# Attention and two mixtures on one core: which queue issues the DMAs inside the first mixture's branches

## The chip, the cores and the metric

One core of a Trainium2 chip runs the whole program in one launch. The metric is the device time of one execution in microseconds (us). Five engines work beside each other: TensorE (PE, matmuls), VectorE (DVE), ScalarE (ACT), GpSimd (POOL) and SyncE (SP, which here only issues DMAs). Each runs its own instruction stream in program order and waits on semaphores for the others. "SPq", "ACTq" and "POOLq" in a profile are those engines' queues of DMA, register, branch and semaphore instructions.

## The reference, cut to what matters

An attention within chunks of 64 tokens gives x, a matrix of N = 2304 tokens by 512. Two mixtures follow.

```
# first mixture: each token goes to one of 8 experts, with a capacity of 2N/8 = 576 tokens an expert
expert = argmax(x @ w_gate)
gate   = softmax(x @ w_gate)[expert]
y[i]   = gate[i] * relu(x[i] @ w1[expert[i]]) @ w2[expert[i]]     # 0 if over capacity
# second mixture: every token through every expert, weighted by P, a matrix normalised 8 times over rows and columns
P   = exp(y @ w2_gate), then 8 x (rows to sum 1, columns to sum 1, times N/8)
out = sum over e of P[:, e] * relu(y @ w21[e]) @ w22[e]
```

How many tokens an expert of the first mixture gets depends on the data, so the kernel decides at run time how many blocks of rows it works on.

## The kernel before, in words

Matrices are split into a high and a low fp16 part and multiplied three times. The first stage (to about 142 us of the profile) is the attention, the routing and the writing of all token rows to a DRAM buffer `xs_d`; it also leaves in `reg_i` the token count `rc` and the first rank `rb` of each expert, and in `gidx` the tokens of each expert. The second stage (142 to about 427 us) is the first mixture. The third stage (to the end, 1868 us) is the second mixture.

The loop of the first mixture (lines 789 to 862) goes over the experts x = 0 to 7 in turn, and each engine takes the instructions in the order in which they are written:

- GpSimd gathers tokens from `xs_d` by indirect DMA (`gather`, line 665): `late`, the third and fourth 128 tokens of expert x, and `rows`, the first 256 tokens of expert x+1. SyncE turns `rows` by two DMA transposes (`turn_dma`, line 674).
- The main block (`blocks(..., main=True)`, line 848) does the first 256 tokens of expert x. TensorE multiplies with w1 (line 718), ScalarE and VectorE make the hidden tiles hh and hl (lines 722, 723), TensorE turns `late` (`turn`, lines 683 to 686, called through `between`) and multiplies with w2 (line 735). Between the pieces, at `sites`, lie the splits of the next expert's weights (`w_split`, lines 216 to 218 and 224, 225, of which part runs on GpSimd), the loads of weights three experts ahead (`load_next`, line 153, on SyncE) and their statistics. For the last expert the sites hold `w_quad` (lines 240 to 250): GpSimd forms sums of the second mixture's first weights, ScalarE and VectorE split them.
- Each 128 rows of the result are written to the DRAM buffer `x2_d` (line 748, 256 KB) and their scale and token number to `rk_d` (line 753, 128 pairs of 8 bytes). The address is `rb + 128 t`, a register, so a write counts as touching any part of the buffer: each write to `x2_d` waits until the one before it has landed, and so with `rk_d`. Before line 748 GpSimd copies the token numbers into the pair (line 707).
- Then come the branches (lines 850 to 862): with more than 256 tokens a block for the third 128 (`Else`, line 862), with more than 384 a block for the third and fourth together (line 852), with more than 512 a loop for what is left (line 854), with a gather in it. In the profiled execution experts 0 and 2 take the block of two, experts 3 and 6 the block of one, experts 1, 4, 5 and 7 none: 16 + 6 blocks of 128 rows in all.
- For the last expert, `heads` (line 771) loads the first 768 rows of `x2_d` for the second mixture: ahead of the main block if these rows are already written (line 811; so it is here), else inside the innermost branch (line 860).

The DMAs of lines 748 and 753 are issued by SyncE, for the last expert by ScalarE; those of `heads` by SyncE. A side of a branch that issues fewer DMAs than the other, or none, makes up for them: it waits on each semaphore that the other side's DMAs would have raised and raises it itself, so that the count is the same behind the branch. These instructions stand in the profile under the lines of the branches (850, 851, 853): `EVENT_SEMAPHORE` on SyncE for the semaphores of SyncE's and ScalarE's DMAs, `INC_SWDGE_SEM` on GpSimd for those of GpSimd's. This text calls them pads.

The second mixture starts with `x_first` (line 930), whose matmuls read `heads` (line 943) and whose results go into tiles on the memory that the first mixture has left (lines 952, 961, 962).

Of the kernel before, what the change touches and what calls it, by code (L numbers as in the profile page):

```python
# [30 lines left out]
def kernel(ctx, tc, q, k, v, w_gate, w1, w2, capacity, w2_gate, w21, w22, out):  # L31
    nc = tc.nc
    B, H, S, D = q.shape
    N, DM = out.shape
    E, _, F = w1.shape
# [19 lines left out]
    x2_d = dram.tile([N + 256, DM], F32, name="x2_d")  # L55
# [11 lines left out]
    def sm(nm, shape, dtype=F32):  # L67
        return small_pool[-1].tile(shape, dtype, tag=nm, name=nm)
# [19 lines left out]
    def pow2_of_sumsq(ssq, log2, h, s, inv):  # L88
        nc.vector.tensor_scalar(out=h, in0=ssq.bitcast(I32), scalar1=24, scalar2=None, op0=ALU.logical_shift_right)
        nc.vector.tensor_scalar(out=s.bitcast(I32), in0=h, scalar1=-float(1 << 23), scalar2=float((189 + log2) << 23),  # L90
                                op0=ALU.mult, op1=ALU.add)
        nc.vector.tensor_scalar(out=inv.bitcast(I32), in0=h, scalar1=float(1 << 23), scalar2=float((65 - log2) << 23),
                                op0=ALU.mult, op1=ALU.add)
# [163 lines left out]
    for i in range(NS):  # L257
        r, done = [], 0
        while done < 256:
            b, s = divmod(i * 256 + done, S)  # L260
            n = min(256 - done, S - s)
# [6 lines left out]
    reg_i = const.tile([128, 2 * E], I32, name="reg_i")  # L268
    gidx = const.tile([128, E, NT], I32, name="gidx")
    NV = 4  # L270
    with ExitStack() as actx:
# [330 lines left out]
        for n in range(NT + 6):  # L602
# [13 lines left out]
            queue = []  # L616
# [6 lines left out]
            for f, lag in order:  # L623
# [5 lines left out]
                queue = queue[share:]  # L629
# [20 lines left out]
    with ExitStack() as cctx:  # L650
# [27 lines left out]
        def turn(rows, tag, bank="y"):  # L678
            xT = cp.tile([128, 2 * KD, 128 * len(rows)], F16, tag=tag, name=tag, bufs=2 if tag == "xT" else 1)
            for n, (idx, kg, xg) in enumerate(rows):  # L680
                p = ps_c.tile([128, 2 * KD, 128], F16, tag=bank, name="p_t", bufs=2 if bank != "p" else 3)
                for kk in range(2 * KD):
                    nc.tensor.transpose(p[:, kk, :], xg[:, kk * 128:(kk + 1) * 128], id16)
                sl = slice(n * 128, (n + 1) * 128)
                nc.scalar.copy(out=xT[:, 0:KD, sl], in_=p[:, 0:KD])
                nc.vector.tensor_copy(xT[:, KD:2 * KD, sl], p[:, KD:2 * KD])
            return xT, rows
# [3 lines left out]
        def blocks(x, pre, nb, row0, sites=(), main=False, between=None):  # L691
            a, b = mats[x, "a"], mats[x, "b"]
            xT, rows = pre
            W = 128 * nb
            sites = list(sites)

            def bank(nm, shape):
                tag, bufs = {"p": ("p", 3), "y": ("y", 2)}[nm] if main else ("c", 2)
                return ps_c.tile(shape, F32, tag=tag, name="p_" + nm, bufs=bufs)

            def site():
                for f in (sites.pop(0) if sites else ()):
                    f()

            tos = [sm("rkt", [128, 2]) for _ in range(nb)]
            for (idx, _, _), to in zip(rows, tos):
                nc.gpsimd.tensor_copy(to[:, 1:2].bitcast(I32), idx)
            hh = cp.tile([128, KF, 256], F16, tag="hh", name="hh", bufs=1)[:, :, 0:W]
            hl = cp.tile([128, KF, 256], F16, tag="hl", name="hl", bufs=1)[:, :, 0:W]
            FG = 512 // W  # L710
            for fg in range(KF // FG):
                p = bank("p", [128, FG, W])
                for f4 in range(FG):
                    f = fg * FG + f4
                    n = 0
                    for w, lo in ((a.hi, 0), (a.hi, KD), (a.lo, 0)):
                        for kk in range(KD):
                            nc.tensor.matmul(p[:, f4, :], lhsT=w[:, kk, f * 128:(f + 1) * 128], rhs=xT[:, lo + kk, 0:W],  # L718
                                             start=(n == 0), stop=(n == 3 * KD - 1))
                            n += 1  # L720
                fs = slice(fg * FG, fg * FG + FG)
                nc.scalar.activation(out=hh[:, fs, :], in_=p, func=AF.Relu)
                nc.vector.scalar_tensor_tensor(out=hl[:, fs, :], in0=p, scalar=0.0, in1=hh[:, fs, :],
                                               op0=ALU.max, op1=ALU.subtract)
                site()
            for t in range(nb):
                idx, kg, _ = rows[t]
                sl = slice(t * 128, t * 128 + 128)
                if t == 0 and between:
                    between()  # L730
                y = bank("y", [128, DM])
                n = 0
                for kk in range(KF):
                    for h, w in ((hh, b.hi), (hh, b.lo), (hl, b.hi)):
                        nc.tensor.matmul(y, lhsT=h[:, kk, sl], rhs=w[:, kk, :], start=(n == 0), stop=(n == 3 * KF - 1))  # L735
                        n += 1
                sq, ssq = cp.tile([128, DM], BF16, tag="sq", name="sq2", bufs=1), sm("ssq2", [128, 1])
                nc.scalar.activation(out=sq, in_=y, func=AF.Square, accum_out=ssq)
                s, inv = sm("x2s", [128, 1]), sm("x2i", [128, 1])
                pow2_of_sumsq(ssq, LX, sm("x2h", [128, 1], I32), s, inv)  # L740

                rhl = cp.tile([128, 2, 2, DM // 2], F16, tag="row", name="row2", bufs=3)
                yh = y.rearrange("p (c n) -> p c n", c=2)
                nc.scalar.activation(out=rhl[:, :, 0, :], in_=yh, func=AF.Copy, scale=s)
                nc.vector.scalar_tensor_tensor(out=rhl[:, :, 1, :], in0=yh, scalar=s, in1=rhl[:, :, 0, :],
                                               op0=ALU.mult, op1=ALU.subtract)
                queue = nc.scalar if x == E - 1 else nc.sync
                queue.dma_start(out=x2_d[bass.ds(row0(t), 128), :],
                                in_=rhl.rearrange("p c l n -> p (c l n)").bitcast(F32))
                to = tos[t]  # L750
                nc.vector.scalar_tensor_tensor(out=to[:, 0:1], in0=kg, scalar=inv, in1=iws[x],
                                               op0=ALU.mult, op1=ALU.mult)
                queue.dma_start(out=rk_d[bass.ds(row0(t), 128), :], in_=to)
                site()
            assert not sites
# [12 lines left out]

        head = []

        def heads():
            for n, (lo, hi) in enumerate(((0, 4), (4, 6))):
                if len(head) < 2:
                    head.append(wpool.tile([128, 4096], F16, tag=f"s{2 + n}", name=f"head{n}").bitcast(F32)
                                .rearrange("p (j c) -> p j c", c=DM))
                nc.sync.dma_start(out=head[n][:, 0:hi - lo, :],
                                  in_=x2_d[lo * 128:hi * 128, :].rearrange("(j p) c -> p j c", p=128))

        def tokens(x, *ts):
            return [gidx[:, x, t:t + 1] for t in ts]  # L780
# [8 lines left out]
        for x in range(E):  # L789
            y = x + 1  # L790
            rc = nc.values_load(reg_i[0:1, x:x + 1], min_val=0, max_val=N)
            rank_engine = mybir.EngineType.Activation if x == E - 1 else mybir.EngineType.SP
            rb = nc.values_load(reg_i[0:1, E + x:E + x + 1], engines=[rank_engine], min_val=0, max_val=N)

            def rank(t):
                return nc.s_assert_within(rb + t * 128, 0, N + 128,
# [2 lines left out]
            def ranks(t0):  # L799
                return lambda t: rb if t0 + t == 0 else rank(t0 + t)  # L800
# [7 lines left out]
                    loads(2, nm)  # L808
            if x == E - 1:
                with tc.If(rc <= N - SB):  # L810
                    heads()

            if y < E:
                for nm in "ab":
# [35 lines left out]
            with tc.If(rc > 256):  # L850
                with tc.If(rc > 384) as cmp:
                    blocks(x, (late_t, late_r), 2, ranks(2))
                    with tc.If(rc > 512):
                        with tc.For_i(4, (rc + 127) // 128, 1) as t:
                            idx = cp.tile([128, 1], I32, tag="idx", name="idx")
                            nc.vector.tensor_copy(idx, gidx[:, x, bass.ds(t, 1)])
                            blocks(x, turn(gather([idx]), "xTl", "c"), 1, lambda _: rank(t))
                        if x == E - 1:
                            with tc.If(rc > N - SB):
                                heads()  # L860
                with cmp.Else():
                    blocks(x, (late_t, late_r[:1]), 1, ranks(2))

# [258 lines left out]
    for x in range(E):  # L1122
# [36 lines left out]
        for s in range(NSB):  # L1159
            hs = [[ep.tile([128, SB], F16, tag=f"{nm}{f}", name=nm) for nm in ("eh", "el")] for f in range(KF)]  # L1160
            n = 0
# [15 lines left out]
            for t in range(6):  # L1177
                j = s * 6 + t
# [13 lines left out]
                if x == E - 1:  # L1192
                    nc.gpsimd.indirect_dma_start(out=out[:, :], out_offset=bass.IndirectOffsetOnAxis(ap=rk[:, j, 1:2].bitcast(I32), axis=0),
                                                 in_=acc[:, j, :], in_offset=None)
# [38 lines left out]
```

## Time and profile before

| | |
|---|---|
| runs of the kernel before | 1873.75, 1872.31, 1871.22 us (median 1872.31) |
| the profiled execution | 1869.98 us |
| its span, first to last instruction | 1868.3 us |
| PE / DVE / ACT / POOL busy, share of the span | 96% / 54% / 39% / 26% |
| mean granted TensorE clock | 0.982 of full speed (2.4 GHz) |

A row of a timeline gives the start and the length of a run of like instructions on one engine, and in square brackets how long the engine was idle before it and what it waited for. A row of the view of one line gives count, shortest, median and longest duration in ns, and the first and last start. Idle time of an engine that is not the bottleneck costs nothing by itself.

### The profile page before, as it was taken

The numbers are of one execution on the slowest core, as the hardware profiler recorded it, in microseconds if no ns is written. First come the engines' busy times: TensorE is split into PE (matmuls) and PEld (weight loads), VectorE is DVE, ScalarE is ACT, GpSimd is POOL, SyncE is SP. The second block draws the span as 40 slices with busy tenths as digits, with TensorE's granted clock in tenths as the row PEclk, the third lists the DMA queues.
The fourth block names the chain that finished last, engine by engine and source line by source line (L and its number), as shares of the span: only waits on it lengthen the run. The fifth ranks groups of instructions, "written<-read, shape, count | busy, mean of one in ns | idle before, by whom it ended". The sixth has DMA issues, their size and how long they took to land.

```text
span 1868.3 us, 27396 instructions
## 1 busy us (share of the span) xinstructions
PE 1785.7 (96%) x10757; PEld 1015.4 (54%) x10757; DVE 1013.1 (54%) x1978; ACT 721.0 (39%) x1310; POOL 479.1 (26%) x494
## 2 busy tenths in 40 slices
PE   7868999888999999999999999999999999999998
PEld 6756666655455555555545555555555555555553
DVE  4896657756566734654464545355534653464432
ACT  7964656644334333541233323233322431242210
POOL 1344336541012310421131113112301321042221
PEclk9988999989999999999999999999999999999999
DMA  9747556833342112130222113112112130212200
GB/s 232 204 154 225 157 177 162 220 112 126 91 121 78 60 45 104 60 105 9 96 85 80 60 47 104 60 60 105 46 60 102 63 105 1 105 59 72 82 34 35
DMA packets 135118, 182.11 MB, mean 97 GB/s; under 512 B 62240, under 2 KB 80752, under 8 KB 134960
## 3 DMA queue, kind: packets, MB, share of 16 engines
q1 hardware_dynamic: 127968, 162.22, 28.1%
q0 software_dynamic: 5360, 17.24, 2.9%
q8 instruction: 98, 1.61, 0.4%
q14 instruction: 60, 0.49, 0.1%
q10 hardware_dynamic: 1632, 0.56, 0.1%
HBM read 149.21 MB, written 23.56 MB: 92 GB/s over the span
## 4 chain that ended last, share of the span: by engine, by line
PE 69%; DVE 4%; ACT 3%; issue 1%; POOL 1%; DMA 0%; POOLq 0%; DVEq 0%
PE p_m L1116 39%; PE p_m L1054 29%; DVE c L1060 1%; ACT eh L1070 1%; DVE el L1071 1%; ACT wsq L164 1%; POOL w L1089 1%; PE p_m L943 0%; ACT m L1079 0%; ACT m L1099 0%; PE p_l L173 0%; DVE w L225 0%; DVE u L1060 0%; ACT w L224 0%; DMA out_dram<-acc,rk 0%
## 5 line engine op out<-in xcount | busy, mean ns | idle before, releaser
L1116 PE MATMUL p_m<-w,eh 128*128 128x512 f16 x2304 | 685.6, 379 | 2.5 <-ACT eh L1070 2.5
L1054 PE MATMUL p_m<-x,w 128*128 128x384 f16 x4032 | 665.1, 327 | 1.7 <-DVE c L1060 1.3
L1054 PEld LDWEIGHTS <-w 128*128 128x128 f16 x4032 | 395.0, 98 | 264.6 <-issue 4.9
L1116 PE MATMUL p_m<-w,el 128*128 128x512 f16 x1152 | 437.0, 379 | 0.0
L1116 PEld LDWEIGHTS <-eh 128*128 128x128 f16 x2304 | 225.2, 98 | 269.0 <-ACT eh L1070 3.7
L1089 POOL TENSOR_TENSOR w<-u,m 128x384 f32<-128x384 f32 x96 | 96.6, 1006 | 971.3 <-DVE u L1060 911.2
L1070 ACT ACTIVATE eh<-c 128x384 f16<-128x384 f32 x384 | 190.3, 518 | 402.3 <-DVE c L1060 402.3
L1190 DVE SCALAR_TENSOR_TENSOR acc<-p_m,cf,acc 128x512 f32<-128x512 f32 x126 | 94.6, 751 | 383.1 <-PE p_m L1116 376.9
L1071 DVE SCALAR_TENSOR_TENSOR el<-c,eh 128x384 f16<-128x384 f32 x384 | 218.3, 570 | 126.7 <-ACT eh L1070 116.1
L1079 ACT COPY m<-p_m 128x384 f32<-128x384 f32 x96 | 44.6, 465 | 400.3 <-PE p_m L1054 400.3
L1116 PEld LDWEIGHTS <-el 128*128 128x128 f16 x1152 | 112.7, 98 | 137.3 <-DVE el L1071 1.8
L718 PEld LDWEIGHTS <-w 128*128 128x128 f16 x1152 | 109.0, 102 | 30.5 <-issue 11.5
L735 PE MATMUL p_y<-w,hh 128*128 128x512 f16 x352 | 106.4, 384 | 0.0
L718 PE MATMUL p_p<-xT,w 128*128 128x256 f16 x768 | 91.3, 282 | 10.5 <-DMA xT<-xg 4.8
L1094 POOL TENSOR_TENSOR c<-u,m 128x384 f32<-128x384 f32 x96 | 95.7, 997 | 1.5 <-DVE u L1060 1.5
L1060 DVE TENSOR_TENSOR u<-p_m,m 128x384 f32<-128x384 f32 x96 | 53.4, 556 | 59.6 <-PE p_m L1054 59.6
L1060 DVE TENSOR_TENSOR c<-p_m,w 128x384 f32<-128x384 f32 x96 | 53.5, 558 | 49.9 <-PE p_m L1054 32.6
L249 ACT ACTIVATE w<-wsum,wsa 128x1024 f16<-128x1024 f32 x32 | 36.6, 1145 | 88.0 <-POOL wsum L243 88.0
L1060 DVE TENSOR_TENSOR u<-p_m,u 128x384 f32<-128x384 f32 x96 | 53.5, 558 | 27.8 <-PE p_m L1054 25.7
L735 PE MATMUL p_y<-w,hl 128*128 128x512 f16 x176 | 67.5, 384 | 1.1 <-issue 1.1
L164 ACT ACTIVATE wsq<-sta 128x1024 bf16<-128x1024 f32 x64 | 67.6, 1056 | 0.9
L225 DVE SCALAR_TENSOR_TENSOR w<-stb,wsb,w 128x1024 f16<-128x1024 f32 x46 | 62.9, 1379 | 6.2 <-ACT w L224 6.1
(236 smaller groups left out, 1663.3 us busy)
## 6 DMA issues: line engine op xcount, KB each, us to landing
x<-xt_d SPq DMA_DIRECT2D x147, 384.0 KB, 4.5
sta<-in_moe_w_dram SPq DMA_DIRECT2D x18, 1024.0 KB, 7.0
stb<-in_moe_w_dram SPq DMA_DIRECT2D x18, 1024.0 KB, 7.3
sta<-in_moe_w_dram SPq DMA_DIRECT2D x28, 512.0 KB, 8.7
stb<-in_moe_w_dram SPq DMA_DIRECT2D x28, 512.0 KB, 12.2
xt_d<-x SPq DMA_DIRECT2D x21, 384.0 KB, 3.1
x_d<-row SPq DMA_DIRECT2D x20, 256.0 KB, 4.6
vbd<-in_v_dram SPq DMA_DIRECT2D x72, 64.0 KB, 4.1
```

The costliest lines, as they stand in the source:

```text
L164: nc.scalar.activation(out=sq, in_=src, func=AF.Square, accum_out=m.mx[:, h:h + 1])
L225: nc.vector.scalar_tensor_tensor(out=m.lo[:, sl, :], in0=m.st[:, sl, :], scalar=m.s, in1=m.hi[:, sl, :], op0=ALU.mult, op1=ALU.subtract)
L718: nc.tensor.matmul(p[:, f4, :], lhsT=w[:, kk, f * 128:(f + 1) * 128], rhs=xT[:, lo + kk, 0:W], start=(n == 0), stop=(n == 3 * KD - 1))
L735: nc.tensor.matmul(y, lhsT=h[:, kk, sl], rhs=w[:, kk, :], start=(n == 0), stop=(n == 3 * KF - 1))
L1054: nc.tensor.matmul(p, lhsT=wt[:, w, lw, kk, :], rhs=xt[:, lx, kk, :], start=(n == 0), stop=(n == 5))
L1060: nc.vector.tensor_tensor(out=c, in0=p, in1=t, op=ALU.add)
L1070: nc.scalar.activation(out=hh[:, sl], in_=src, func=AF.Relu)
L1071: nc.vector.scalar_tensor_tensor(out=hl[:, sl], in0=src, scalar=0.0, in1=hh[:, sl], op0=ALU.max, op1=ALU.subtract)
L1089: nc.gpsimd.tensor_tensor(out=Q["w"], in0=Q["u2"], in1=Q["m5"], op=ALU.add)
L1094: nc.gpsimd.tensor_tensor(out=Q["c22"], in0=Q["u3"], in1=Q["m5"], op=ALU.add)
L1116: nc.tensor.matmul(y, lhsT=h[:, t * 128:(t + 1) * 128], rhs=w[:, kk, :], start=(n == 0), stop=(n == 3 * KF - 1))
L1190: nc.vector.scalar_tensor_tensor(out=acc[:, j, :], in0=y, scalar=coefs[x][:, j:j + 1], in1=acc[:, j, :], op0=ALU.mult, op1=ALU.add)
```

## The change

In the branches every DMA is issued by GpSimd; the main blocks' writes of all experts, the last one's too, by SyncE. `heads` is issued by GpSimd at both places. The first rank `rb` is loaded into registers of SyncE and of GpSimd for every expert (before: SyncE, for the last expert ScalarE). SyncE then has no instruction inside a branch.

```diff
-                queue = nc.scalar if x == E - 1 else nc.sync
+                queue = nc.sync if main else nc.gpsimd
                 queue.dma_start(out=x2_d[bass.ds(row0(t), 128), :], ...
                 queue.dma_start(out=rk_d[bass.ds(row0(t), 128), :], in_=to)
...
-        def heads():
+        def heads(queue):
...
-                nc.sync.dma_start(out=head[n][:, 0:hi - lo, :],
-                                  in_=x2_d[lo * 128:hi * 128, :].rearrange("(j p) c -> p j c", p=128))
+                queue.dma_start(out=head[n][:, 0:hi - lo, :],
+                                in_=x2_d[lo * 128:hi * 128, :].rearrange("(j p) c -> p j c", p=128))
...
-            rank_engine = mybir.EngineType.Activation if x == E - 1 else mybir.EngineType.SP
-            rb = nc.values_load(reg_i[0:1, E + x:E + x + 1], engines=[rank_engine], min_val=0, max_val=N)
+            rb = nc.values_load(reg_i[0:1, E + x:E + x + 1], engines=[mybir.EngineType.SP, mybir.EngineType.Pool],
+                                min_val=0, max_val=N)
...
                 with tc.If(rc <= N - SB):
-                    heads()
+                    heads(nc.gpsimd)
...
                             with tc.If(rc > N - SB):
-                                heads()
+                                heads(nc.gpsimd)
```

## Rows read from the trace of the kernel before

**Rows 1.** Busy time by stretch; behind the engines: PEclk, DMA share, GB/s.

```profile
142.00:427.00 285.00, 253.36 (x1854) 173.41 (x1854) 177.90 (x332) 160.43 (x252) 130.27 (x98) 0.95 0.62 174
...
353.00:358.00 5.00, 5.00 (x25) 3.62 (x25) 0.00 (x0) 0.00 (x0) 2.82 (x2) 0.50 1.02 193
```

**Rows 2.** Waits of SP's queue from 142 to 428: total, times, longest.

```profile
SPq L748 <- DMA x_d<-row: 44.5, 8, 13.0
```

**Rows 3.** Timeline of SP: the first row write inside each branch that is taken.

```profile
194.66 0.33 SPq L748 DMA_DIRECT2D x_d<-row  x1
...
268.61 0.33 SPq L748 DMA_DIRECT2D x_d<-row  x1
...
310.11 0.34 SPq L748 DMA_DIRECT2D x_d<-row  x1
...
394.98 0.34 SPq L748 DMA_DIRECT2D x_d<-row  x1
```

**Rows 4.** Pads under line 850, the outermost branch, on SP and on POOL.

```profile
L850 SPq EVENT_SEMAPHORE  x26: 17/17/17, 236.8 to 429.7; - x26
...
L850 POOLq INC_SWDGE_SEM  x4: 757/1022/1180, 215.7 to 413.3; - x4
```

**Rows 5.** GpSimd's row writes in the attention stage (line 421), with their landing.

```profile
L421 POOL DMA_DIRECT2D xs_d<-row x15: 540/562/765, 36.1 to 127.8; - x15
...
DMA to landing us min/median/max: 2.0/3.5/7.2
```

**Rows 6.** Gathers (line 665), with landing: all; the one at 198; those at 358 to 363.

```profile
L665 POOL DMA_INDIRECT xg<-xs_d,gidx x32: 942/954/1234, 142.2 to 380.4; - x32
...
DMA to landing us min/median/max: 3.4/7.4/11.3
...
DMA to landing us min/median/max: 4.1/4.1/4.1
...
DMA to landing us min/median/max: 5.3/6.1/7.2
```

**Rows 7.** Timeline of POOL: weight splits, gathers, sums for the second mixture.

```profile
203.83 2.85 POOL L217 TENSOR_SCALAR stb<-stb,wsb 128x1024 f32<-128x1024 f32 x1
...
217.55 1.02 POOL L665 DMA_INDIRECT xg<-xs_d,gidx  x1 [2.02 <-issue]
218.88 0.96 POOL L665 DMA_INDIRECT xg<-xs_d,gidx  x1 [0.30 <-DVE wmxb L166]
...
358.25 1.03 POOL L665 DMA_INDIRECT xg<-xs_d,gidx  x1 [2.35 <-issue]
...
397.20 0.73 POOL L240 TENSOR_TENSOR wsum<-sta 128x256 f32<-128x256 f32 x1
```

**Rows 8.** Timeline of PE: turning `late` of experts 1 to 6 (L683), start of expert 6 (L718).

```profile
207.17 1.31 PE L683 MATMUL p_t<-id,xg 128*128 128x128 f16 x16
...
230.39 0.61 PE L683 MATMUL p_t<-id,xg 128*128 128x128 f16 x8
...
277.84 1.31 PE L683 MATMUL p_t<-id,xg 128*128 128x128 f16 x16
...
311.96 1.30 PE L683 MATMUL p_t<-id,xg 128*128 128x128 f16 x16
...
335.12 0.61 PE L683 MATMUL p_t<-id,xg 128*128 128x128 f16 x8
...
352.89 5.28 PE L718 MATMUL p_p<-xT,w 128*128 128x256 f16 x24 [4.81 <-DMA xT<-xg]
...
366.52 1.06 PE L683 MATMUL p_t<-id,xg 128*128 128x128 f16 x16
```

**Rows 9.** Timeline of ACT: the last row write of the first mixture, and the first copy of the second.

```profile
425.58 0.34 ACTq L748 DMA_DIRECT2D x_d<-row  x1
...
429.77 0.86 ACT L952 CAST x<-p_m 128x384 f16<-128x384 f32 x2 [5.01 <-SPq L850]
```

**Rows 10.** Landing of ScalarE's two row writes (line 748).

```profile
DMA to landing us min/median/max: 2.0/2.1/2.1
```

## The prediction, made before the changed kernel was run

> **What bounds the kernel now.** I read the busy time by stretch first. From 142 to 427 us, the first mixture, TensorE is busy 253 of 285 us [rows 1]; the second mixture, three quarters of the time, holds nothing that the change touches except its start. So the change can take at most some 30 us of waits out of the first mixture, and what it adds there counts in full where TensorE ends up waiting. Second, the waits of SyncE's queue and its timeline: a row write waits for the landing of the row write before it, 44.5 us in 8 places [rows 2]. The first write inside each taken branch (experts 0, 2, 3, 6) goes out at 194.66, 268.61, 310.11 and 394.98 [rows 3]. Today SyncE sits through that, and nothing of GpSimd's is behind it. Third, GpSimd's timeline: its gathers for the next expert stand ahead of its weight split, and the split and the pads of the branches ahead of the next gathers [rows 7]. Fourth, TensorE's timeline: 10.8 to 11 us into each main block it turns `late`, so both of its gathers must have landed [rows 8]. At expert 2 they are only just in time: issued at 217.55 and 218.88, wanted at 230.39 [rows 7, 8].
>
> **What the change does to SyncE.** It leaves the branches: the 12 writes in taken branches (6 rows, 6 pairs), its 2 loads of `heads` and all its pads. Under line 850 alone there are 26 pads, that is 6 for each of experts 1, 4 and 5, which take no branch, and 8 for expert 7: one pad for every DMA of the other side [rows 4]. Gain at two places. (a) Expert 6 starts at 352.89 after a wait of 4.81 us for its transposes [rows 8], which SyncE had issued late, behind pads; they can go out earlier. (b) The second mixture's first copy at 429.77 waits for SyncE's last pad [rows 9]; that tile also needs the last row's landing, 425.58 + 2.05 = 427.63 [rows 9, 10], so at most 2.1 us come back there. ScalarE also loses 4 DMA issues, which lay beside TensorE's work: nothing, and SyncE, idle then, issues them as early; if it did not, a row would be late by its issue, 0.3 us.
>
> **What it does to GpSimd.** It gets the 12 writes, the 2 loads of `heads`, a second register load per expert, and the pads, and all of it lies ahead of the next expert's gathers. Prices:
> - A row write: 0.56 us of issue, 0.9 with the register work that SyncE's queue shows between a row and its pair (0.67 from start to start; estimate); landing 3.5 us, from 2.0 to 7.2 [rows 5]. A pair has no GpSimd row of its shape; I take the same. `heads` are six such blocks: between 0.6 us an issue (1.2) and 0.56 a block (3.4); I take 1.8, since one issue carries several blocks.
> - A pad: 0.76 to 1.18 us on GpSimd today [rows 4], against 0.02 on SyncE. I take 0.95 with its gap, and one per DMA, as SyncE's count shows. Today GpSimd pads only the gather in the loop, one at a time. With the change: 7 where no branch is taken (4 writes, 2 in the loop, the gather), 5 after the block of one, 3 after the block of two. The lower bound is one pad instruction for all, the upper 1.18 each.
> - The two register loads: today pad end to first gather is 217.55 - 215.7 - 0.76 = 1.1 us [rows 4, 7]; with the second 1.5 (estimate).
> - Gathers follow each other at 1.25 us (1.33 at 217.55 [rows 7]). Landing: 4.1 with quiet DMA queues, 7.4 (the median of all) beside weight loads, 6.1 for those at 358; the bounds are the shortest and the longest of all, 3.4 and 11.3 [rows 6].
> - GpSimd's split with its wait for ScalarE: 203.83 to 215.7, 11.9 us [rows 4, 7]; I take 11.7.
>
> **The sum**, by the delay of TensorE at each turn of `late` (its second half is wanted 0.6 us behind the row's start):
> - Expert 0 to 1. Row at 194.66, landed 3.5 later, second row 198.2, its pair done 199.7; 3 pads 2.9, loads 1.5: first gather 204.1, second lands 204.1 + 1.25 + 4.1 = 209.4. Wanted 207.8. **+1.6**.
> - 1 to 2. Four gathers from 204.1 end at 209.1, split 11.7, 7 pads 6.7, loads 1.5: 229.0; second lands at 237.6 (7.4, weights in flight). Wanted 231.0 + 1.6. **+5.0**.
> - 2 to 3. 268.61 + 3.5, pair done 273.6, 3 pads, loads: 278.0; landing 5 (queues just drained): 284.2 against 278.5. **+5.7**.
> - 3 to 4. 310.11, pair done 311.6, 5 pads 4.8, loads: 317.9; 324.1 against 312.6. **+11.5**, the largest.
> - 4 to 5. From 317.9: gathers 5, split 11.7, 7 pads, loads, 1.25 and 7.4: 351.4 against 335.7 + 11.5. **+4.2**.
> - 5 to 6. Today's gathers at 358.25 have one pad ahead; 6 more and the load make 6.1: second lands 358.25 + 6.1 + 1.25 + 6.2 = 371.8 against 367.1. **+4.7**. This is where gain (a) goes: an earlier start of expert 6 meets `late` even less ready, so I count (a) as nothing.
> - 6 to 7. 394.98, pair done 396.5, 5 pads, loads: 402.8; two gathers 405.3; `heads` 407.1, copies 0.3. The sums for the second mixture start at 407.4, today at 397.20 [rows 7], and ScalarE's and VectorE's splits behind them hold the hidden tiles of the same queues. **+10.2**.
> - Start of the second mixture: gain (b), **-2.1**; expert 7's 8 pads (some 8 us behind the sums, which ended about 413) finish before the last row has landed.
>
> Together **+40.8**: 1869.98 (the profiled execution: 1868.3 span and 1.7 around it) becomes 1910.8. The median of the runs is 2.3 above that execution, so I predict **1913**. Within the sum nothing is added for the clock: after the wait of 4.81 us the granted share was 0.50, that is 1.2 GHz, over 353 to 358 [rows 1], and 24 matmuls took 5.28 [rows 8], about half of it lost. Such a loss after each new wait is partly work that GpSimd, being late, would have made TensorE wait for anyway; it belongs to the upper end.
>
> The rows show a GpSimd write issue of 0.54 to 0.77 us beside VectorE's work [rows 5]. The Trainium skill, "SBUF — State Buffer", section "SBUF: two separate sides", says that GpSimd cannot write its descriptors while VectorE holds the ports the two share; by its example (about 620 ns alone, 3100 overlapped) 14 issues could cost 35 us more. The longest issue of any gather, 1.23 us [rows 6], speaks against that here.
>
> **Rivals.**
> 1. Pads are cheap: one instruction raises all semaphores of a side (1.1 us a branch). Then by the same steps +0, +0, +4.0, +7.8, 0, 0, +6.5, -2.1 = +16: **1888**. For it: nothing in the trace shows two GpSimd pads in a row. Against: SyncE's 26.
> 2. GpSimd falls behind for good: pads at 1.18, gathers beside weight loads at 11, half speed after five waits of over 4 us (2.5 each, 12): about 60: **1932**. For it: the pads grow along the trace to 1.18.
> 3. Faster: SyncE's pads were what mattered. Gains (a) 4.8 and (b) 2.1, nothing lost: **1865**. The place is GpSimd's first gather behind a taken branch; it decides whether its second lands by 207.8, 278.5 and 312.6. That needs gathers that go out ahead of the branch's writes. Against: GpSimd keeps the written order, and the row write goes out at 310.11 by itself.
> 4. No change, **1872**: only issue time moves. The rows price 12 writes at 0.56 for 0.33 each, 3 us on engines that wait anyway; for this the write's wait would have to hold nothing behind it, and at 310.11 it holds the gathers wanted at 311.96 [rows 3, 8]. The Trainium skill, "DMA: Bandwidth & Descriptors", section "Issuing engines are not separate DMA queues", says that the choice of the issuing engine saves only the sequencer's time to start a DMA, usually small; by that it would be this case.
>
> **How the numbers follow.** Forecast 0.58; rival 1 0.20, rival 2 0.15, rival 3 0.05, rival 4 0.02. The range takes in rivals 1 and 2 with their spread: 1885 to 1938. A measurement of this kernel tells about 0.2%, 4 us, from no change. Faster is rival 3, 0.05; the same is rival 4, 0.02; slower the rest, 0.93.
>
> **What would show it.** Right: TensorE waits at line 683 for `DMA xg` at experts 2 to 6, longest at expert 4; runs of `INC_SWDGE_SEM` of 3 to 7 in a row at the joins; no instruction of SyncE under lines 850 to 853; the sums of line 240 start some 10 us later into expert 7. Wrong: the turns of `late` as close to their block's start as today, or a single pad per join, or second-mixture matmuls that start later than the last row's landing plus 2 us, which would mean that GpSimd's pads hold the join.

## The result, and the profile after

| | before | after |
|---|---|---|
| median of the runs taken together | 1873.03 us (4 runs) | 1890.76 us (4 runs) |
| the profiled execution | 1869.98 us | 1888.27 us |
| its span | 1868.3 us | 1886.6 us |
| mean granted TensorE clock | 0.982 | 0.977 |

The change makes the kernel slower: ratio 1.0106, 95% interval 1.0088 to 1.0125. The medians of the table differ by 17.7 us, 0.95%. Forecast were +40.8 us and 1913, with a range from 1885 to 1938. The sign and the range held; the size was less than half of the forecast, and close to the +16 of rival 1.

**Where the time went.** The busy time by stretch, kernel after (columns as in [rows 1]):

```profile
142.00:443.00 301.00, 256.08 (x1854) 173.97 (x1854) 178.33 (x331) 161.06 (x252) 135.42 (x112) 0.93 0.58 164
...
318.00:324.00 6.00, 5.86 (x27) 3.11 (x28) 0.85 (x2) 1.17 (x2) 5.92 (x4) 0.53 0.90 189
374.00:379.00 5.00, 5.00 (x20) 2.41 (x21) 2.01 (x4) 0.58 (x1) 4.91 (x5) 0.58 0.66 159
```

The first mixture now lasts to 443 instead of 427, with the same 1854 matmuls. TensorE's busy time makes 2.7 of these 16 us (the clock, below); the rest is waiting. What TensorE waited for in that stage, total, times and longest, first the kernel before (142 to 450 us):

```profile
PE p_t L683 <- DVE hl L723: 6.8, 4, 3.7
PE p_m L943 <- SPq L850: 6.1, 1, 6.1
PE p_p L718 <- issue: 5.6, 3, 2.0
PE p_t L683 <- DMA xg<-xs_d,gidx: 4.9, 2, 4.5
PE p_p L718 <- DMA xT<-xg: 4.8, 1, 4.8
```

and then the kernel after:

```profile
PE p_t L683 <- DMA xg<-xs_d,gidx: 10.9, 6, 4.6
PE p_t L683 <- DVE hl L723: 10.9, 3, 6.6
PE p_p L718 <- issue: 10.6, 5, 5.3
PE p_t L683 <- DVE w L225: 5.4, 1, 5.4
PE p_m L943 <- DVEq L850: 4.3, 1, 4.3
```

The waits in which `late` is turned (line 683) grow from 4.9 + 6.8 to 10.9 + 10.9 + 5.4 us, that is by 15.5; the wait for transposes (4.8) is gone, the start of the second mixture waits 1.8 less, and "issue" grows by 5.0. That makes 13.9 of the 18.3 us between the spans; whether its 5.0 of "issue" belong to the change is open (see the run with later weight loads). The clock adds some 2.4: 6 us at 0.53 and 5 us at 0.58 behind two of the new waits lose 2.8 and 2.1, and the 5 us at 0.50 of before [rows 1] lost 2.5 (estimates from these windows, in which the clock is near the lower of its two levels, 1.2 GHz). Some 2 us are in none of these.

GpSimd's timeline behind the branches of experts 0, 3 and 6:

```profile
191.46 0.64 POOL L748 DMA_DIRECT2D x_d<-row  x1 [21.69 <-DVE rkt L751]
192.23 0.56 POOL L753 DMA_DIRECT2D rk_d<-rkt  x1
196.86 0.54 POOL L748 DMA_DIRECT2D x_d<-row  x1 [4.08 <-DVEq L853]
197.60 0.54 POOL L753 DMA_DIRECT2D rk_d<-rkt  x1 [0.20 <-issue]
202.15 1.03 POOL L665 DMA_INDIRECT xg<-xs_d,gidx  x1 [4.01 <-DMA rk_d<-rkt]
...
308.35 0.65 POOL L748 DMA_DIRECT2D x_d<-row  x1 [18.44 <-DMA x_d<-row]
309.13 0.56 POOL L753 DMA_DIRECT2D rk_d<-rkt  x1
312.09 1.30 POOL L665 DMA_INDIRECT xg<-xs_d,gidx  x1 [2.40 <-issue]
...
407.97 0.65 POOL L748 DMA_DIRECT2D x_d<-row  x1 [22.34 <-DVE rkt L751]
408.75 0.56 POOL L753 DMA_DIRECT2D rk_d<-rkt  x1
411.96 1.03 POOL L665 DMA_INDIRECT xg<-xs_d,gidx  x1 [2.65 <-issue]
...
414.27 1.59 POOL L776 DMA_DIRECT2D head<-x_d  x2
...
416.06 0.78 POOL L240 TENSOR_TENSOR wsum<-sta 128x256 f32<-128x256 f32 x1
```

The gathers stand right behind the branch's writes, as forecast, but only 3.0 to 4.6 us behind the last pair (from start to start). TensorE's timeline at the turns of `late` (compare [rows 8]), at the longest hole of "issue" (394.59), and at the starts of expert 6 (358.15) and of the second mixture (443.22):

```profile
208.14 0.62 PE L683 MATMUL p_t<-id,xg 128*128 128x128 f16 x8 [1.15 <-DMA xg<-xs_d,gidx]
...
278.25 0.62 PE L683 MATMUL p_t<-id,xg 128*128 128x128 f16 x8 [1.11 <-DMA xg<-xs_d,gidx]
...
317.99 2.21 PE L683 MATMUL p_t<-id,xg 128*128 128x128 f16 x16 [5.39 <-DVE w L225]
...
345.84 1.06 PE L683 MATMUL p_t<-id,xg 128*128 128x128 f16 x16
...
358.15 2.78 PE L718 MATMUL p_p<-xT,w 128*128 128x256 f16 x24 [0.90 <-PEq L850]
...
372.02 1.04 PE L683 MATMUL p_t<-id,xg 128*128 128x128 f16 x8 [2.86 <-DMA xg<-xs_d,gidx]
373.95 1.04 PE L683 MATMUL p_t<-id,xg 128*128 128x128 f16 x8 [0.90 <-DMA xg<-xs_d,gidx]
...
394.59 5.24 PE L718 MATMUL p_p<-xTc,w 128*128 128x128 f16 x56 [5.31 <-issue]
...
422.23 1.01 PE L683 MATMUL p_t<-id,xg 128*128 128x128 f16 x8 [6.60 <-DVE hl L723]
426.57 1.01 PE L683 MATMUL p_t<-id,xg 128*128 128x128 f16 x8 [3.33 <-DVE hl L723]
443.22 1.65 PE L943 MATMUL p_m<-id,head 128*128 128x128 f16 x14 [4.29 <-DVEq L850]
```

The longest wait for gathers is at expert 4, 5.39 us. The view puts it down to VectorE's line 225, but the gather decides it: the three gathers issued from 312.09 to 314.97 land in

```profile
DMA to landing us min/median/max: 5.0/5.4/5.9
```

The first of them takes the 5.9, and 312.09 + 5.9 is 317.99, where TensorE goes on. Expert 5 has no such wait, expert 6 starts without its 4.81 us for transposes and pays 2.86 + 0.90 at the turn instead. In expert 7 the sums of line 240 start at 416.06, which is 11.2 us into the expert instead of 5.1, and TensorE waits 9.9 us for hidden tiles there, 4.7 before.

**The pads.** The lines of the branches, kernel after (compare [rows 4]):

```profile
L850 SPq COMPARE_BRANCH  x8: 34/46/53, 181.0 to 444.0; - x8
...
L850 POOLq INC_SWDGE_SEM  x4: 837/1234/1484, 219.6 to 432.0; - x4
...
L851 POOLq INC_SWDGE_SEM  x2: 1154/1278/1403, 309.3 to 408.9; - x2
...
L853 POOLq INC_SWDGE_SEM  x2: 813/914/1014, 198.3 to 269.2; - x2
```

The kernel before has, beside the four of [rows 4]:

```profile
L851 POOLq INC_SWDGE_SEM  x2: 900/1018/1136, 288.9 to 376.7; - x2
...
L853 POOLq INC_SWDGE_SEM  x2: 703/764/825, 170.8 to 251.7; - x2
```

Eight joins, eight pads, in both kernels: one per join, however many DMAs the other side has. In the kernel after they last 4 x about 1.2, 2 x 1.28 and 2 x 0.91, some 9 us together, in the kernel before 7.5. By the prediction's count there were to be 45 of 0.95, 43 us.

### The profile page after: what moved, and what is told of

Its sections match the earlier page's. It is cut to its first block, busy times and chain, and to the rows that moved or that the text cites. A ratio compares the mean times of both kernels' runs of the same rounds, so it can differ in the third digit from the quotient of the medians.

```text
span 1886.6 us, 27418 instructions
## 1 busy us (share of the span) xinstructions
PE 1789.2 (95%) x10757; PEld 1016.1 (54%) x10757; DVE 1013.4 (54%) x1978; ACT 721.2 (38%) x1310; POOL 484.9 (26%) x508
## 4 chain that ended last, share of the span: by engine, by line
PE 68%; DVE 3%; ACT 3%; issue 1%; POOL 1%; DMA 0%; POOLq 0%; DVEq 0%; ACTq 0%
PE p_m L1116 39%; PE p_m L1054 29%; DVE c L1060 1%; ACT eh L1070 1%; DVE el L1071 1%; ACT wsq L164 1%; POOL w L1089 1%; ACT m L1079 0%; DMA x_d<-row 0%; DVE u L1060 0%; PE p_l L173 0%; ACT m L1099 0%; DVE w L225 0%; PE p_m L943 0%; ACT w L224 0%
## 5 line engine op out<-in xcount | busy, mean ns | idle before, releaser
L718 PEld LDWEIGHTS <-w 128*128 128x128 f16 x1152 | 107.8, 101 | 29.6 <-issue 17.0
L718 PE MATMUL p_p<-xT,w 128*128 128x256 f16 x768 | 89.1, 277 | 8.2 <-issue 5.2
```

## The experiments

Theory 1: the time is lost because work of GpSimd for the next expert stands behind the branch's rows in its queue. Theory 2, the first rival: the price of issues and pads on GpSimd loses it, wherever the rest stands. The expectations in us were written against 1873 for the kernel before; beside the experiments it took 1864.8, 1867.2 and 1866.1 (medians of 23, 27 and 35 runs), so the ratios to it are what is compared. On this scale the change itself is 1.0106.

**The gathers ahead of the branch.** In the kernel after, and in the kernel before:

```diff
-            if x > 0:
-                late = gather(tokens(x, 2, 3))
-                rows = gather(tokens(x + 1, 0, 1)) if y < E else None
             cur, pre = pre, turn_dma(rows) if y < E else None
...
             late_t, late_r = nxt[0]
+            if y < E:
+                late = gather(tokens(y, 2, 3))
+                rows = gather(tokens(y + 1, 0, 1)) if y + 1 < E else None
             with tc.If(rc > 256):
```

(The gather in the loop gets a buffer of its own.)

> The changed kernel with the gathers for the next expert issued ahead of the branch instead of behind it. Theory 1 (order on GpSimd's queue): the added time is that these gathers stand behind the branch's row writes and the join's pad; ahead of them they land before TensorE wants them, the 16 us of waits for gathers fall under 3, the 4.8 us wait for transposes stays away, and the time is 1866 to 1876, against 1890 for the change. Theory 2 (price of GpSimd's DMAs): it is the issues and pads themselves, wherever the gathers stand; then 1885 to 1892, with the waits on VectorE and on the sums of line 240 larger.

> The kernel before with the same gathers ahead of the branch, rows still on SyncE. Theory 1: the 4.9 us of waits for gathers go, the 4.8 us wait for the transposes of expert 6 stays, since SyncE's queue makes it: 1867 to 1872, at most 5 us below before and 0 to 6 us below or above the changed kernel with the gathers moved. Theory 2: the same, since nothing is added to GpSimd; this run only gives the base line for the other.

Measured: kernel after with the gathers moved 1.0033 (1.0014 to 1.0053), kernel before with them moved 1.0017 (1.0002 to 1.0032). TensorE's waits, kernel after with the gathers moved:

```profile
PE p_p L718 <- issue: 10.8, 9, 5.0
PE p_t L683 <- DVE hl L723: 10.5, 4, 5.0
PE p_t L683 <- DMA xg<-xs_d,gidx: 7.2, 3, 4.5
...
PE p_m L943 <- DVEq L850: 4.3, 1, 4.3
```

Of the 7.2 us the 4.5 belong to the very first turn, which every kernel here has; 2.7 are left of the change's, and there is no wait for transposes. About 7 of the 10.6 thousandths come back, which theory 2 excludes (1.006 to 1.010 by its numbers). The rest is larger than theory 1 said (at most 1.002): the waits on VectorE of expert 7 stay. In the kernel before the same move gains nothing; its interval even lies just above 1. The 4.9 us that I expected to go there are nearly all the first turn's, which the move does not touch; its other gathers were in time.

**The branches' rows on ScalarE.** `nc.gpsimd` becomes `nc.scalar` for the rows of the branches, `heads` stays with SyncE, the rank is loaded for ScalarE.

> The branches' rows issued by ScalarE, heads by SyncE, main rows by SyncE as in the change. Theory 1: nothing stands ahead of the gathers, so no added wait at line 683; ScalarE waits for VectorE's row and the landing ahead, which holds only work of the same branch and the first copies of the next block: 1866 to 1880. Theory 2 (GpSimd's price): also near before. A third theory, that it costs to take the rows out of SyncE's queue at all (their order against the main rows): 1885 to 1892.

Measured: 1.0090 (1.0072 to 1.0109). I had taken ScalarE for harmless, and it loses about as much as GpSimd. Its timeline behind expert 0's branch, and TensorE's in expert 1:

```profile
195.62 0.34 ACTq L748 DMA_DIRECT2D x_d<-row  x1
196.27 1.83 ACTq L753 DMA_DIRECT2D rk_d<-rkt  x1
199.61 0.60 ACT L722 ACTIVATE hh<-p_p 128x512 f16<-128x512 f32 x1 [4.80 <-DMA rk_d<-rkt]
```

```profile
194.10 2.78 PE L718 MATMUL p_p<-xT,w 128*128 128x256 f16 x24 [1.12 <-issue]
...
208.28 0.61 PE L683 MATMUL p_t<-id,xg 128*128 128x128 f16 x8 [2.55 <-DVE hl L723]
```

The next block's first product was ready at 194.10 + 2.78 = 196.88; ScalarE takes it up at 199.61, behind the pair of the old block. TensorE's waits for hidden tiles at line 683 are 14.6 us in this trace against 6.8 before. So the loss is not GpSimd's alone: ScalarE too holds its own work for the next expert behind the branch's rows. Theory 1 would stand in this wider form, theory 2 (which had this run near before) does not. For ScalarE this is read from the trace; no run moves its work ahead of the rows. The time also lies in the range of the third theory, that it costs to take the rows out of SyncE's queue at all. What speaks against that one is the run with gathers and sums moved, below: there the rows have left SyncE too, and nothing is lost.

**`heads` back on SyncE.** `heads(nc.sync)` at both places of the kernel after.

> The change without its part on heads: the two loads of heads stay with SyncE. Theory 1: GpSimd's two issues of 0.8 us stand ahead of the sums of line 240, which start 1.6 us earlier, and that is all: 1886 to 1890. Rival: the heads are what holds expert 7 (waits of 6.6 and 3.3 us at line 683): 1879 to 1884.

Measured: 1.0108 (1.0090 to 1.0126), no different from the change. The sums of line 240 start 9.7 us into expert 7 instead of 11.2, as expected, and TensorE's first wait there is 5.02 us instead of 6.60, but no gain shows in the time. The rival, that `heads` are what holds expert 7, falls.

**More DMAs on the untaken side.** The row write of the loop's body, which this input never enters, is cut into 8:

```diff
+                for c in range(parts):
+                    cs = slice(c * DM // parts, (c + 1) * DM // parts)
...
-  blocks(x, turn(gather([idx]), "xTl", "c"), 1, lambda _: rank(t))
+  blocks(x, turn(gather([idx]), "xTl", "c"), 1, lambda _: rank(t), parts=8)
```

> The changed kernel, with the row write of the loop's body (which this input never enters) cut into 8 writes, so that each of the 8 joins has 7 more GpSimd DMAs of an untaken side to make up for. By the prediction's count (one pad of 0.95 us per DMA) GpSimd gets 6.7 us more ahead of the gathers of each expert, and the time rises by 15 us or more, to a ratio of 1.018 or above. If one instruction raises all semaphores of a side, the pads stay one per join and the ratio is the change's own, 1.009 to 1.0125.

Measured: 1.0170 (1.0149 to 1.0191), between the two. The joins (the lines are 2 higher here):

```profile
L852 POOLq INC_SWDGE_SEM  x4: 847/1240/1494, 223.8 to 441.2; - x4
...
L855 POOLq EVENT_SEMAPHORE  x10: 17/43/5062, 199.9 to 272.7; - x10
L855 POOLq INC_SWDGE_SEM  x2: 800/904/1007, 204.0 to 277.8; - x2
...
L1230 POOLq INC_SWDGE_SEM  x4: 680/760/844, 295.4 to 416.3; - x4
```

Still one pad per join and of the same length (847/1240/1494 against 837/1234/1484), with four more of 0.68 to 0.84 us, by their times two in each of the two blocks of one: the count of pads, on which the forecast's size rested, is refuted. That the time rose all the same, both theories miss. Behind expert 2's block of two the trace shows a wait of 5.06 us ahead of the pad; in the kernel after, the waits ahead of these pads last 43 ns at most. The wait ends when the branch's own last pair has landed: issued at 272.16, landed 5.5 us later, pad at 277.8. The first gather then stands 8.4 us behind the start of that pair, against 3.7 in the kernel after (7.0 against 4.6 behind expert 0's block). Why the join waits there with more DMAs on the untaken side is not shown; I take it that there are more semaphores to wait for, those of these writes among them.

**The weight loads later.** Theory C was that the holes ("issue" at line 718) are TensorE's instructions brought in beside the weight loads; `load_next()` is called behind the branch instead of behind the first row (in the kernel before that is behind SyncE's rows of the branch, too).

```diff
-            behind = [load_next]
+            behind = []
...
                     blocks(x, (late_t, late_r[:1]), 1, ranks(2))
+            load_next()
```

> The changed kernel with the gathers ahead of the branch, and with the weight loads of the expert after next issued by SyncE behind the main block's second row instead of behind its first, so that they no longer run while TensorE enters the branch. Theory C (instructions of the branch are brought in beside these loads): TensorE's waits of line 718 for nothing that the profile shows fall from 10.8 us to 4 to 6, the 5.0 us hole at 386 to about 2: 3 to 6 us below the kernel with the gathers moved alone, ratio to before 0.999 to 1.001. Rival: these holes cost the same wherever the loads are: ratio 1.002 to 1.005.

> The kernel before with the weight loads behind the main block's second row alone. Theory C: its holes under line 718 are 5.6 us together, of which 2.0 in expert 6 stand beside these loads, so 0 to 2 us: ratio 0.998 to 1.001. If the loads are then late for the sums of the weights or hold SyncE's transposes: 1.002 to 1.008.

Measured: 1.0049 (1.0029 to 1.0069) with the gathers moved, 1.0031 (1.0017 to 1.0045) in the kernel before. The issue waits of the first hardly move (10.4 against 10.8 us). Those of the second fall from 5.6 to 3.3, while its waits for transposes rise from 4.8 to 7.8. Neither is faster, so these runs do not bear theory C out, and what makes the holes stays open. A hole also differs between executions. With expert 6 as in the kernel before, and a ratio of 1.0000 (the kernel with expert 7's rows on SyncE, at the end of this section), the hole of expert 6 that was 2.03 us in the profile of before is

```profile
382.88 5.34 PE L718 MATMUL p_p<-xTc,w 128*128 128x128 f16 x56 [4.97 <-issue]
```

So the 3.3 us more at 394.59 need not come from the change. Whether any of the 5.0 does is open: the holes of line 718 sum to 6.1 to 11.4 us in the profiles of the eight kernels in which the branches' rows have left SyncE, and to 3.3 to 8.0 in the six others, with one profile each.

**The first sums ahead of the branch too.** In expert 6, ahead of the branch (and the two steps are left out of expert 7's sites):

```diff
+            if y == E - 1:
+                wsums += [xw.tile([128, 4, 2, 128], F32, name=f"wsum{i}") for i in range(2)]
+                for q in range(2):
+                    w_quad(E, q, 0)
             with tc.If(rc > 256):
```

This was run on the kernel after with gathers and loads moved, on the kernel after with gathers moved alone, and on the kernel before:

> As the kernel with gathers ahead of the branch and later loads, and with the first two groups of GpSimd's sums for the second mixture (line 240) also ahead of expert 6's branch. Theory 1, that all of GpSimd's work for the next expert is held by the branch's rows: the waits of 5.0 and 3.3 us in expert 7 on VectorE fall under 4 together, 3 to 5 us below the kernel without this part: ratio to before 0.996 to 0.999. Rival: these waits are ScalarE's and VectorE's own work in expert 7 (before has 4.7 of them): 0 to 1 us, ratio 0.999 to 1.001.

> The changed kernel with both gathers and first sums ahead of the branch, weight loads where they were. Theory 1: against the gathers alone (ratio 1.0033) the 8.4 us of waits in expert 7 become under 3: ratio 0.999 to 1.001, so all of the loss is given back and the change by itself is worth about nothing. Rival, a part of the loss is the price of the rows on GpSimd wherever the rest stands: 1.002 to 1.0035.

> The kernel before with GpSimd's first two groups of sums for the second mixture ahead of expert 6's branch, nothing else. Theory 1 says that work for the next expert is late because it stands behind the branch; in the kernel before GpSimd issues nothing in the branch but still starts these sums only in expert 7, and TensorE waits 4.7 us there on VectorE. If the sums set that wait: it falls under 1.5, expert 7 is 4 to 5.6 us shorter, ratio 0.9965 to 0.9985. Rival, ScalarE's and VectorE's own splits set it: ratio 0.999 to 1.001.

Measured: 1.0010 (0.9993 to 1.0027), 0.9989 (0.9974 to 1.0004) and 0.9985 (0.9967 to 1.0004). The first lies above the range that I gave it, but I gave it from a kernel without the sums that I expected at 1.000 and that took 1.0049; the sums ahead gave back 3.9 thousandths there, and 4.4 where the loads stay. In the kernel before, where they should gain 1.5 to 3.5, it is 1.5, not clear of noise. TensorE's waits, kernel after with gathers and sums moved:

```profile
PE p_t L683 <- DMA xg<-xs_d,gidx: 4.9, 2, 4.5
PE p_t L683 <- DVE hl L723: 3.7, 3, 1.6
```

The 10.5 us on VectorE fell to 3.7, those for gathers to 0.4 beside the first turn. With the whole change kept, its 12 writes, `heads`, pads and register loads on GpSimd, the loss is gone, and it stands level with the kernel before that has the same sums ahead (0.9985); gathers alone gained nothing there (1.0017), and both together were not run in it. So the price of these DMAs on GpSimd is nothing that this measurement can tell (the intervals reach 0.0015 to 0.0019 to each side, some 3 us); within that, the order is all of it.

**The third part alone, and the change for expert 7 alone.** `queue = nc.sync` throughout the kernel before; and, on the kernel before with the sums ahead (the "first kernel of this group" of its expectation), `queue = nc.sync if main or x < E - 1 else nc.gpsimd`.

> The kernel before with expert 7's rows issued by SyncE instead of ScalarE: the change's third part alone (its branch side stays with SyncE too). All theories: ratio 0.9985 to 1.0015; then with heads worth nothing too (1.0108 without them) the whole loss is the branches' rows.

> The first kernel of this group with the change kept for expert 7 alone (main rows on SyncE, its branch's rows on GpSimd), where no gathers for a next expert stand behind the branch. Theory 1: no loss from it, and SyncE passes the last join earlier: the 6.1 us wait at the start of the second mixture falls to about 4.3; 0 to 2 us below the first kernel of this group. Rival, rows on GpSimd cost by themselves: 1 to 3 us above it.

Measured: 1.0000 (0.9983 to 1.0016) and 0.9978 (0.9963 to 0.9993). The third part is worth nothing that shows; with `heads` worth nothing as well, the branches' rows, with the register loads that go with them, carry the 1.0106. The last kernel is the only one of all whose interval lies below the kernel before. It is not told apart from the two at 0.9985 and 0.9989, and the wait at the start of the second mixture did not fall as I expected (6.3 us). `heads` on SyncE still leaves that engine two pads at the last join, at 423.4, where TensorE goes on at 423.44.

## Why the prediction was right or wrong

**What bounds the kernel**: right. The second mixture took 1441 us before (from 427.7 to the span's end) and 1443 after (from 443.2); 15.5 of the 18.3 us were added before it, most of it waiting of TensorE in the first.

**The mechanism**: right, and shown. Gathers and sums behind the branch's rows were late (the gathers at experts 1, 3, 4 and 6, where the text named 2 to 6), the gathers longest at expert 4; with both written ahead of the branch, the loss is gone.

**The size: the step that failed is the count of pads**, "one per DMA, as SyncE's count shows". The count came from SyncE's 26 instructions of 0.02 us, and nothing in the trace of before showed two of GpSimd's in a row; it showed exactly one per join [rows 4], because there was one DMA to make up for, and I chose the larger reading. Measured: one of 0.81 to 1.48 us per join, and with 7 more DMAs on the untaken side still one. The kernel before had the same eight, so the change added some 1.6 us of pads in all, where the forecast has some 25 us of delay from them (40.8 against rival 1's 16). Rival 1 is the same sum with this one term changed; it gave +16, and +17.7 came. That these two are so close is in part luck: the table below shows that rival 1 misses by 2.9 at expert 3 and has nothing at expert 6, and in the traces the waits that it is about (line 683, the transposes, the start of the second mixture) come to 8.9; the clock's 2.4 and the 5.0 of holes, which it does not have, bring the rest near.

**The terms**, forecast and measured wait:

| turn | forecast | with one pad (rival 1) | measured |
|---|---|---|---|
| expert 1 | +1.6 | 0 | 1.15 |
| expert 2 | +5.0 | 0 | none for gathers |
| expert 3 | +5.7 | +4.0 | 1.11 |
| expert 4 | +11.5 | +7.8 | 5.39, and about 2.8 of clock |
| expert 5 | +4.2 | 0 | 0 |
| expert 6 | +4.7 | 0 | 3.76, and about 2.1 of clock |
| expert 7 | +10.2 | +6.5 | 9.93, where before had 4.7 |
| second mixture | -2.1 | -2.1 | -1.8 |

At expert 3's branch the first gather was forecast 317.9 - 311.6 = 6.3 us behind the end of the pair's issue, and came 312.09 - 309.69 = 2.4 us behind it; the pads make 4.8 - 1.15 = 3.65 of these 3.9.

**Gain (a)**, "nothing": right on balance. The 4.81 us did come back at the start of expert 6, and the turn of `late` took them again, 3.76 and the clock. **The sums of line 240** start 6.1 us later into expert 7, not some 10.

**The clock**, "nothing is added": wrong by some 2.4 us net.

**Left out**: a gather behind a branch of two also waits for the landing of the last pair, 4.01 us ahead of 202.15 with the pad inside it. **Wrong in the letter**: "no instruction of SyncE under lines 850 to 853"; its branches remain (40 ns each), its pads are gone. **Misread**: `late` is not turned 10.8 to 11 us into each main block; at expert 6 it is 366.52 - 352.89 = 13.6, at the lower clock. No term rests on it.

**The issue price** of 0.56 us was right: 0.54 to 0.65 for rows and pairs. The 35 us, an estimate from the example in the Trainium skill ("SBUF — State Buffer", section "SBUF: two separate sides"), did not come; no issue of a row was longer than 0.65. The longest issue of a gather was 1.96, against 1.23 before.

**Rival 4**: the Trainium skill ("DMA: Bandwidth & Descriptors", section "Issuing engines are not separate DMA queues") says that starting DMAs on several engines at once saves only the sequencer's time to start them. The runs agree where nothing waits behind the DMA (expert 7's rows 1.0000, the change with gathers and sums moved 0.9989) and differ where something does (1.0106 on GpSimd, 1.0090 on ScalarE): GpSimd is idle 18.44 to 22.34 us ahead of the rows at 191.46, 308.35 and 407.97, and what is written behind them waits too.

## What to carry to other kernels

Before a DMA is moved to another engine, list what that engine issues behind it and who wants it when; the wait of the DMA, not its issue, is the price. Where work for the next stage can be written ahead of the DMA that waits, do that first; here the choice of engine then cost nothing that could be measured. When a count is carried from one engine to another, look for a place in the trace where the second engine shows that count.

## What was not expected of the hardware

The length of the pad `INC_SWDGE_SEM` went with the number of DMAs that GpSimd had issued in this mixture, not with the number that it made up for. In the kernel before it grows from 0.70 us, with 6 gathers ahead of it, to 1.18, with all 32; in the kernel after from 0.81, with 10 DMAs ahead, to 1.48, with 46. With the rows on ScalarE, where GpSimd issues the 32 gathers alone, the eight pads have the lengths of before within 0.005 us, though the last starts at 430.0 instead of 413.3. This is read from the traces; no run changes that number by itself.

The holes of TensorE in a branch, in which the profile shows nothing that it waits for, were 2.03 us in the profile of before and 4.97 in that of a kernel whose expert 6 is the same.
